# An attention and mixer kernel: one more start-up tile, a weight piece moved, and a small add put on GpSimd

## The chip, the cores and the metric

The kernel runs on one core of one Trainium2 chip. The metric is device time in microseconds for one execution. Three runs of the kernel before took 833.48, 834.04 and 835.19 us; the median is 834.04 us. The profile comes from one execution of its own, which took 833.98 us; the span from its first to its last instruction is 832.2 us, and 1.8 us lie around it.

## What is computed

Windowed attention over 8 batches, 8 heads, 576 positions and 64 channels a head, followed by a mixer with two dense parts. Cut to what matters:

```python
scores = (q @ k.T) / 8                       # every (batch, head)
mask   = 0 <= i - j < 64                     # each row sees at most 64 keys
attn   = softmax(where(mask, scores, -1e9))  # divides by (row sum + 1e-09)
x      = (attn @ v), heads side by side      # 8 x 576 x 512, float32
h      = relu(x.T @ w_tok1) @ w_tok2         # over the positions: 576 -> 256 -> 576
u      = x + h.T
out    = u + relu(u @ w_ch1) @ w_ch2         # over the channels: 512 -> 1536 -> 512
```

[...]

## The kernel before

**Stages.** The attention is cut into 36 tiles of 128 rows. Two batches make nine tiles, and a tile holds two blocks of 64 positions. While tile i is finished, tile i+1 goes through its softmax and tile i+2 has its scores computed, all in one loop over i from -1 to 36. The channel part of the mixer follows and is almost TensorE alone. Products of 32-bit accuracy are made of pairs of rounded numbers, a high part (`xhi`, `w1hi`, `t2hi`, `hhi`) and the rest (`xlo`, `w1lo`, `t2lo`, `hlo`), so a value is split before TensorE uses it.

**One tile.** TensorE (PE) computes the scores `s` (line 274, function `qk`). The scores of one tile take two buffers, and these are free again when the softmax of the tile before has read its own. VectorE (DVE) adds the mask and takes the row maximum, in eight instructions of line 289; four make `softmax(i, 0)` and four `softmax(i, 1)`. ScalarE (ACT) takes the exponentials and the row sums `sum` (line 297). TensorE transposes them into `pp` (line 304), ACT copies this to `pt` (line 306), and TensorE multiplies by `v` into `xp` (line 316, function `av`). Function `recip` makes `ri`, the reciprocal of the row sums, and `norm` (line 330) multiplies `xp` by it on DVE. `split_x` makes `xhi` on ACT and `xlo` on GpSimd (POOL, line 104). `tok1` (line 361) multiplies the split rows by `w_tok1` into `h`; a batch needs five of these tiles. When a batch is complete, ACT takes `hhi` (line 372) and DVE `hlo` (line 381), and the pieces of `tok2` (lines 402 and 409) follow in later tiles. The two buffers of `h` are free for the next batch when `hlo` has been taken.

**Weights.** The 28 first pieces of the weights are converted inside the loop, at most one a tile, as the table `JOBS` says. Pieces 0 to 3 are `w_tok1` (320 columns), 4 to 6 `w_tok2`, the rest `w_ch1` and `w_ch2` (384 columns). A piece is loaded by SyncE's queue (`job_load`), goes through lines 196, 198 and 199 on DVE (`job_convert_a`) and through 208, 210 and 211 on DVE and an add of line 213 on POOL into `w` (`job_convert_b`). Some tiles later `job_finish` splits it: the high part on ACT, the rest on POOL, but on DVE for `w_tok2` (line 104 again).

**Order.** Each engine works its instructions off in the order in which the program writes them. The constant `N_START` sets the order within a tile. In tiles below it, both halves of the next softmax stand at the tile's start, both halves of the exponentials follow one another, waiting pieces are finished before `tok1`, and the conversion stands whole at the tile's end. In tiles from `N_START` on, the second half of the softmax, of the exponentials and the two halves of a conversion are spread over the tile. `N_START` is 6: tiles 0 to 5 have the first manner. Tile 7 runs `tok1` for two tiles (`TOK1_SLOW`), the fifth and the sixth, and needs their `xhi` and `xlo`; `tok2` needs all seven pieces of `w_tok1` and `w_tok2` finished from tile 7 on.

Of the kernel before, what the change touches and what calls it, by code (L numbers as in the profile page):

```python
# [16 lines left out]
ALU = mybir.AluOpType  # L17
# [9 lines left out]
TPP = 9  # L27
# [12 lines left out]
N_FIRST = 28  # L40


JOBS = {i: 1 if 0 <= i < 7 or i == 12 or i > 6 and i % TPP not in (0, 3, 5) else 0 for i in range(-1, 37)}
PIECES = {7: (0, 2), 22: (1, 0), 23: (1, 0), 31: (1, 0), 32: (1, 0), 33: (1, 0), 34: (1, 0), 35: (3, 0), 36: (2, 1)}

TOK1_FROM, TOK1_SLOW, TOK2_FROM = 2, 7, 7

N_START = 6

NX = 4  # L50
NCHUNK = TOK // CHUNK
# [32 lines left out]
def mixer_kernel(ctx: ExitStack, tc: tile.TileContext, qh, kh, vh, wt1, wt2, wc1, wc2, out):  # L84
    nc = tc.nc
# [13 lines left out]
    def split(eng_hi, eng_lo, hi, lo, src):  # L99
        if eng_hi is nc.scalar:  # L100
            nc.scalar.copy(hi, src)  # L101
        else:
            eng_hi.tensor_copy(hi, src)
        eng_lo.tensor_sub(lo, src, hi.bitcast(F32))  # L104
# [18 lines left out]
    with ExitStack() as actx:  # L123
# [8 lines left out]
        def load_k(i):  # L132
            p, t = divmod(i, TPP)
            if t in (0, 4):
                b = 2 * p + (t == 4)
                kbs[b] = pq.tile([P, NBLK + 1, H // 2, BLK], F32, name=f"k{b}", tag="k", bufs=2)
                if b != 0:
                    nc.sync.dma_start(kbs[b], kh[b])

        def load_q(i):  # L140
            qr = pq.tile([P, H // 2, 2, BLK], F32, name=f"q{i}", tag="q", bufs=5)
            nc.sync.dma_start(qr, qh[i])
            loaded[i] = [qr, None]

        def load_v(i):
            vt = pq.tile([P, 2, H, D], F32, name=f"v{i}", tag="v", bufs=3)
            nc.sync.dma_start(vt, vh[i])
            loaded[i][1] = vt
# [89 lines left out]
        def job_convert_b():  # L238
            if to_convert_b:
                n, part = to_convert_b.pop(0)  # L240
                to_finish.append((n, to_f32_b(*part)))
# [3 lines left out]
        def job_finish():  # L245
            if to_finish:
                n, w = to_finish.pop(0)
                finished.add(n)
                src, hi, lo, o, m = jobs[n]
                if hi is None:  # L250
                    nc.sync.dma_start(w2_dram[:, o:o + m], w)
                else:
                    eng = nc.vector if src is wt2 or n >= N_FIRST else nc.gpsimd
                    split(nc.scalar, eng, hi[:, o:o + m], lo[:, o:o + m], w)
                    if src is wt1 and o + m == 5 * DT:
                        for c, r in enumerate((top, bottom)):
                            nc.gpsimd.tensor_copy(t1z[r, c], t1lo[r, 4 * DT:].bitcast(F32))
# [34 lines left out]
        def softmax_exp(i, u):  # L292
            e = e_sb[i, u]
            nm, sm = st[i]
            for h in range(4):
                g = 2 * h + u
                nc.scalar.activation(e[:, h], e[:, h], AF.Exp, bias=nm[:, g:g + 1], scale=-1.0,  # L297
                                     accum_out=sm[:, g:g + 1])
# [22 lines left out]
        def recip(i):  # L321
            _, sm = st.pop(i)
            ri = pa.tile([P, H], F32, name=f"ri{i}", tag="ri", bufs=2)
            nc.vector.scalar_tensor_tensor(out=ri, in0=sm, scalar=1e-9, in1=sm, op0=ALU.add, op1=ALU.max)
            nc.vector.reciprocal(ri, ri)
            return ri

# [61 lines left out]
        def tok2(b, half, ct, hh):  # L389
            assert len(finished) >= 7  # L390
            p, odd = divmod(b, 2)
            base = p * TPP + (5 if odd else 0)
            s0, n = (0, 256) if half == 0 else (256, 320)
            up = ps.tile([P, 512], F32, name=f"up{b}_{half}_{ct}", tag=up_tags[0][0], bufs=up_tags[0][1])
            up_tags.append(up_tags.pop(0))
            cs = slice(ct * P, (ct + 1) * P)
            segs = [(base + 2 * half + j, ident, j * P) for j in range(2)]
            if half == 1:

                segs.append((p * TPP + 4, swapped if odd else ident, 256))  # L400
            for j, (i, perm, o) in enumerate(segs):
                nc.tensor.matmul(up[:, o:o + P], xs[i][:, cs], perm,  # L402
                                 start=(j == 0), stop=False, is_transpose=True, skip_group_check=True)
            k = 0
            for tt in range(NTT):
                hi, lo = hh[tt]
                for hx, w in ((hi, t2hi), (hi, t2lo), (lo, t2hi)):
                    k += 1
                    nc.tensor.matmul(up[:, :n], hx[:, cs], w[:, tt * S + s0:tt * S + s0 + n],  # L409
                                     start=False, stop=(k == 6), skip_group_check=True)  # L410
            if ct == 0:
                ust[b, half] = pa.tile([P, NCT, 320], F32, name=f"u{b}_{half}", tag="ust", bufs=2)
            us = ust[b, half]
            nc.scalar.copy(us[:, ct, :n], up[:, :n])
            if ct == NCT - 1:
                stores.append((us, b * S + s0, n))
                if b >= B - 2:
                    store_u()
# [28 lines left out]
        def run_pieces(k):  # L447
            for _ in range(min(k, len(pieces))):
                tok2(*pieces.pop(0))
# [22 lines left out]
        for i in range(-1, NT + 1):  # L472
            if 0 <= i and i + 2 < NT:
                load_v(i + 2)
            if 3 <= i + 3 < NT:
                load_q(i + 3)
            if i + 4 < NT:
                load_k(i + 4)
            store_u()
            n_jobs = JOBS[i]  # L480
            if i == NT - 1:
                up_tags += [("s", 2), ("pt", 2)]
            have = len(pieces)
            n_pieces = PIECES.get(i, (1, 1) if i >= TOK2_FROM else (0, 0))
            pts = []
            if 0 <= i < NT:
                pts.append(pt_transpose(i, 0))
                if i < NT - 1:
                    pts.append(pt_transpose(i, 1))
            if i + 1 < NT:  # L490
                softmax(i + 1, 0)
            if i < N_START:
                softmax(i + 1, 1)
            if 0 <= i < NT:
                ri = recip(i)
            if i > N_START:
                while to_finish:
                    job_finish()
            for n in tok1_plan.get(i + 1, ()):
                last_use = n - NX + ((n - NX) % TPP == 4)  # L500
                if n < i and last_use not in tok1_plan.get(i, ()):
                    split_x(n)
            if i + 1 < NT:
                softmax_exp(i + 1, 0)
            run_pieces(min(have, n_pieces[0]))
            have = min(have, len(pieces))
            if i >= N_START:
                for _ in range(n_jobs):
                    job_convert_a()
            if i == NT - 1:  # L510
                pts.append(pt_transpose(i, 1))
            if N_START <= i < NT - 1:
                softmax(i + 1, 1)
            if i < N_START:
                softmax_exp(i + 1, 1)
                while to_finish:
                    job_finish()
            for n in tok1_plan.get(i, ()):
                tok1(n)
            if N_START <= i < NT - 1:  # L520
                softmax_exp(i + 1, 1)
            if i >= N_START:
                for _ in range(n_jobs):
                    job_convert_b()
            if 0 <= i < NT:
                norm(i, av(i, pts), ri)
            finish_h_low()
            if i < N_START:
                for _ in range(n_jobs):
                    job_convert_a()  # L530
                    job_convert_b()
            if i + 2 < NT:
                qk(i + 2)
            for n in tok1_plan.get(i + 1, ()):
                if n not in xhl:
                    split_x(n)
            run_pieces(min(have, n_pieces[1]))
            while to_load and len(to_convert) < 2 and i < NT - 2:
                job_load()
            if i == NT - 1:  # L540
                while to_convert or to_convert_b or to_finish:
                    job_convert_a()
                    job_convert_b()
                    job_finish()
                qctx.close()
                pu = uctx.enter_context(tc.tile_pool(name="pu", bufs=1, side="right", reuse_waits="tile"))
                ul = {0: load_u(0, pu)}
# [396 lines left out]
```

## Time and profile before

| what | value |
|---|---|
| median of three runs | 834.04 us |
| time of the profiled execution | 833.98 us |
| its span | 832.2 us |
| PE busy | 812.4 us, 98% |
| DVE busy | 508.7 us, 61% |
| ACT busy | 337.5 us, 41% |
| POOL busy | 105.9 us, 13% |
| PE busy from 0 to 65 us | 50.97 us |
| PE busy from 65 to 250 us (rest of the attention) | 184.62 us |
| mean granted TensorE clock | 0.993 |

A row of the profile names the line of the kernel, the engine, the operation, the tile written and the tiles read, and its start and length. The number in brackets behind it is how long its engine sat idle before it, and what ended that. A busy share is a mean over stages with different limits: the first 65 us of this kernel look unlike all that follows, and times below are counted from the span's start. Tile 0 begins at about 8 us and tile 7 ends at about 65 us.

### The profile page before, as it was taken

The numbers are of one execution on the slowest core, as the hardware profiler recorded it, in microseconds if no ns is written. First come the engines' busy times: TensorE is split into PE (matmuls) and PEld (weight loads), VectorE is DVE, ScalarE is ACT, GpSimd is POOL, SyncE is SP. The second block draws the span as 40 slices with busy tenths as digits, with TensorE's granted clock in tenths as the row PEclk, the third lists the DMA queues.
The fourth block names the chain that finished last, engine by engine and source line by source line (L and its number), as shares of the span: only waits on it lengthen the run. The fifth ranks groups of instructions, "written<-read, shape, count | busy, mean of one in ns | idle before, by whom it ended". The sixth has DMA issues, their size and how long they took to land.

```text
span 832.2 us, 15257 instructions
## 1 busy us (share of the span) xinstructions
PE 812.4 (98%) x5860; PEld 678.7 (82%) x5860; DVE 508.7 (61%) x1372; ACT 337.5 (41%) x1014; POOL 105.9 (13%) x110
## 2 busy tenths in 40 slices
PE   7879999999999999999999999999999999999998
PEld 5658888888888878888888888878888878888886
DVE  5987977788782993774435535267625277525252
ACT  7868888888874440331212202033202032202020
POOL 3533443443430000000000000000000000000000
PEclk9979999999999999999999999999999999999999
DMA  9847778588536538633605442424543334532002
GB/s 348 276 138 240 230 249 270 188 274 287 191 122 192 179 85 242 203 112 114 202 1 196 170 190 89 139 91 165 167 184 110 119 112 172 173 150 89 1 1 101
DMA packets 69672, 136.51 MB, mean 164 GB/s; under 512 B 7008, under 2 KB 39264, under 8 KB 67680
## 3 DMA queue, kind: packets, MB, share of 16 engines
q1 hardware_dynamic: 67488, 133.71, 47.4%
q10 hardware_dynamic: 2112, 1.84, 0.7%
q8 instruction: 46, 0.75, 0.4%
q14 instruction: 26, 0.21, 0.1%
HBM read 104.66 MB, written 30.87 MB: 163 GB/s over the span
## 4 chain that ended last, share of the span: by engine, by line
PE 82%; DVE 10%; ACT 3%; issue 2%; DMA 2%; POOLq 0%; SPq 0%; POOL 0%; DVEq 0%; ACTq 0%
PE gp L843 19%; PE op L631 11%; PE gp L623 8%; PE up L409 5%; PE h L361 5%; PE op_4a L631 4%; PE op_2b L631 4%; PE op_2a L631 4%; PE op_0b L631 4%; PE op_0a L631 4%; PE op_4b L631 4%; PE s L274 3%; PE xp L316 3%; PE pp L304 3%; PE up L402 2%
## 5 line engine op out<-in xcount | busy, mean ns | idle before, releaser
L843 PE MATMUL gp<-m,w1hi 128*128 128x512 f32 x504 | 155.4, 389 | 0.7 <-DVE x L851 0.7
L297 ACT ACTIVATE e<-e,nm 128x128 f32<-128x128 f32 x288 | 112.3, 397 | 12.4 <-DVE nm L289 12.3
L843 PEld LDWEIGHTS gp<-m,w1hi 128*128 128x128 f32 x504 | 94.5, 188 | 20.9 <-DVE x L851 1.5
L843 PE MATMUL gp<-m,w1lo 128*128 128x512 f32 x252 | 98.0, 389 | 0.0
L610 ACT ACTIVATE ghi<-x 128x512 fp32r<-128x512 f32 x54 | 34.2, 632 | 119.8 <-DVE x L853 68.3
L289 DVE CUSTOM_DVE_ANT_0 e<-s,mask 128x128 f32<-128x128 f32 x288 | 65.3, 284 | 11.3 <-PE s L274 11.1
L847 ACT COPY x<-gp 128x512 f32<-128x512 f32 x18 | 10.4, 578 | 143.7 <-PE gp L843 143.7
L611 DVE SCALAR_TENSOR_TENSOR glo<-x,ghi 128x512 fp32r<-128x512 f32 x54 | 37.4, 692 | 38.1 <-ACT ghi L610 38.1
L610 ACT ACTIVATE ghi<-gp 128x512 fp32r<-128x512 f32 x50 | 29.9, 598 | 70.3 <-PE gp L623 70.3
L623 PE MATMUL gp<-ulo,w1hi 128*128 128x512 f32 x144 | 56.0, 389 | 0.0
L623 PE MATMUL gp<-uhi,w1hi 128*128 128x512 f32 x144 | 56.0, 389 | 0.0
L297 ACT ACTIVATION_READ_ACCUMULATOR e<-e,nm 128x1 f32 x288 | 56.0, 195 | 0.0
L623 PE MATMUL gp<-uhi,w1lo 128*128 128x512 f32 x144 | 56.0, 389 | 0.0
L843 PEld LDWEIGHTS gp<-m,w1lo 128*128 128x128 f32 x252 | 47.3, 188 | 9.9
L274 PE MATMUL s<-k,q 64*64 64x128 f32 x1152 | 43.2, 280 | 10.4 <-DVE nm L289 4.1
L611 DVE SCALAR_TENSOR_TENSOR glo<-gp,ghi 128x512 fp32r<-128x512 f32 x50 | 34.4, 689 | 25.4 <-ACT ghi L610 25.3
L631 PE MATMUL op<-glo,w2hi 128*128 128x512 f32 x128 | 49.8, 389 | 0.0
L631 PE MATMUL op<-ghi,w2hi 128*128 128x512 f32 x128 | 49.8, 389 | 0.0
L631 PE MATMUL op<-ghi,w2lo 128*128 128x512 f32 x128 | 49.8, 389 | 0.0
L316 PEld LDWEIGHTS xp<-v,pt 128*64 128x64 f32 x1152 | 36.6, 138 | 13.3 <-ACT e L297 9.4
L104 POOL TENSOR_TENSOR xlo<-x,xhi 128x512 fp32r<-128x512 f32 x32 | 41.3, 1292 | 38.8 <-ACT xhi L101 38.5
L274 PEld LDWEIGHTS s<-k,q 64*64 64x64 f32 x1152 | 33.4, 135 | 14.5 <-issue 10.6
(160 smaller groups left out, 1835.0 us busy)
## 6 DMA issues: line engine op xcount, KB each, us to landing
v<-vh SPq DMA_DIRECT2D x36, 512.0 KB, 4.1
w1hi<-w1s SPq DMA_DIRECT2D x18, 896.0 KB, 4.6
w1lo<-w1s SPq DMA_DIRECT2D x18, 896.0 KB, 6.4
raw<-wc SPq DMA_DIRECT2D x32, 384.0 KB, 4.4
q<-qh SPq DMA_DIRECT2D x36, 256.0 KB, 4.6
k<-kh SPq DMA_DIRECT2D x7, 1280.0 KB, 7.8
out<-uf SPq DMA_DIRECT2D x35, 256.0 KB, 2.8
uf<-u_dram SPq DMA_DIRECT2D x8, 1024.0 KB, 9.2
```

Of the source, the lines that this page charges most:

```text
L104: eng_lo.tensor_sub(lo, src, hi.bitcast(F32))
L274: nc.tensor.matmul(so, qt[r, j, half], kbs[b][r, n:n + 2, j], start=True, stop=True)
L289: nc.vector.tensor_tensor_reduce(out=e[:, h], in0=s[:, h], in1=mk, scale=-scale, scalar=MAX_F32, op0=ALU.add, op1=ALU.min, accum_out=nm[:, ...
L297: nc.scalar.activation(e[:, h], e[:, h], AF.Exp, bias=nm[:, g:g + 1], scale=-1.0, accum_out=sm[:, g:g + 1])
L316: nc.tensor.matmul(xp[half * BLK:(half + 1) * BLK, h], pts[h % 2][:, h // 2, half * BLK:(half + 1) * BLK], vt[:, half, h], start=True, sto ...
L361: nc.tensor.matmul(h_ps[b][tt], w[:, o + tt * P:o + (tt + 1) * P], x, start=first and n == 0, stop=last and n == len(combos) - 1)
L409: nc.tensor.matmul(up[:, :n], hx[:, cs], w[:, tt * S + s0:tt * S + s0 + n], start=False, stop=(k == 6), skip_group_check=True)
L610: nc.scalar.activation(hi, src, AF.Relu)
L611: nc.vector.scalar_tensor_tensor(out=lo, in0=src, scalar=0.0, in1=hi.bitcast(F32), op0=ALU.max, op1=ALU.subtract)
L623: nc.tensor.matmul(gp, w[:, w1_at(ft, ct)], x[:, ct], start=(k == 0), stop=(k == 3 * NCT - 1))
L631: nc.tensor.matmul(op, w[:, ct, ft], x[:, cols], start=(first and k == 0), stop=(last and k == 3 * len(gs) - 1), skip_group_check=not (fir ...
L843: nc.tensor.matmul(b, w[:, at], c[:, h, t], start=(n < 4 and k == 0), stop=(k == 5), skip_group_check=True)
```

## The change

Three edits. The first makes tile 6 a tile of the first manner (`N_START` goes from 6 to 7), and adds a `job_finish` to tile 7, so that pieces 5 and 6 of the weights, which tile 7 finished together, are finished in tile 6 and tile 7. The second takes the conversion out of tile 7 and gives one to tile 18, which had none; the pieces between them are converted by one tile's place later. The third makes the first step of `recip`, the add of 1e-9 to the 128 by 8 sums, an instruction of POOL instead of DVE; the reciprocal stays on DVE.

```diff
-JOBS = {i: 1 if 0 <= i < 7 or i == 12 or i > 6 and i % TPP not in (0, 3, 5) else 0 for i in range(-1, 37)}
+JOBS = {i: 1 if 0 <= i < 7 or i in (12, 18) or i > 7 and i % TPP not in (0, 3, 5) else 0 for i in range(-1, 37)}
-N_START = 6
+N_START = 7
         def recip(i):
             _, sm = st.pop(i)
             ri = pa.tile([P, H], F32, name=f"ri{i}", tag="ri", bufs=2)
-            nc.vector.scalar_tensor_tensor(out=ri, in0=sm, scalar=1e-9, in1=sm, op0=ALU.add, op1=ALU.max)
+            nc.gpsimd.tensor_scalar_add(ri, sm, 1e-9)
             nc.vector.reciprocal(ri, ri)
             return ri
...
             if i + 1 < NT:
                 softmax_exp(i + 1, 0)
+            if i == N_START:
+                job_finish()
             run_pieces(min(have, n_pieces[0]))
```

On DVE, from the reciprocal of tile 6 (`ri_843`, now `ri_848`) to the multiplication `x` of the same tile. `c` and `r` belong to piece 6 of the weights, `e_1` is the second half of tile 7's softmax. First before, then now (now the second half of the softmax stands ahead of these rows, and the conversion is the last of them).

```order
L325 RECIPROCAL ri_843<-ri_843 128x8
L196 TENSOR_SCALAR c_854<-raw_710 128x384
L198 TENSOR_SCALAR c_854<-c_854 128x384
L199 TENSOR_SCALAR c_854<-c_854 128x384
L289 ISA e_1_858,nm_836<-s_1_799,mask_90 128x128
...
L208 SCALAR_TENSOR_TENSOR c_854<-raw_710,c_854 128x384
L210 TENSOR_SCALAR r_875<-c_854 128x384
L211 SCALAR_TENSOR_TENSOR r_875<-raw_710,r_875 128x384
L330 TENSOR_TENSOR x_898<-xp_881,ri_843 128x512
L381 SCALAR_TENSOR_TENSOR hlo_0_900<-h_0_449,hhi_0_867 128x512
L381 SCALAR_TENSOR_TENSOR hlo_1_902<-h_1_450,hhi_1_869 128x512
```

```order
L325 RECIPROCAL ri_848<-ri_848 128x8
L104 TENSOR_TENSOR t2lo<-w_793,t2hi 128x384
L330 TENSOR_TENSOR x_890<-xp_873,ri_848 128x512
L381 SCALAR_TENSOR_TENSOR hlo_0_892<-h_0_449,hhi_0_869 128x512
L381 SCALAR_TENSOR_TENSOR hlo_1_894<-h_1_450,hhi_1_871 128x512
L196 TENSOR_SCALAR c_896<-raw_710 128x384
L198 TENSOR_SCALAR c_896<-c_896 128x384
L199 TENSOR_SCALAR c_896<-c_896 128x384
L208 SCALAR_TENSOR_TENSOR c_896<-raw_710,c_896 128x384
L210 TENSOR_SCALAR r_900<-c_896 128x384
L211 SCALAR_TENSOR_TENSOR r_900<-raw_710,r_900 128x384
```

The six conversion steps moved behind the multiplication and the two `hlo`, and a `t2lo`, which waits for ACT, moved ahead of them.

On POOL, two pieces of the difference: tiles 3 and 4, then tiles 6 and 7. `w_901` (`w_876` before) is piece 6, `xlo_852` and `xlo_925` (`xlo_847` and `xlo_923`) the low parts of tiles 5 and 6, which `tok1` in tile 7 reads.

```order
 L213 TENSOR_TENSOR w_481<-r_480,c_476 128x320
+L324 TENSOR_SCALAR ri_536<-sum_421 128x8
 L104 TENSOR_TENSOR xlo_540<-x_474,xhi_539 128x512
 L104 TENSOR_TENSOR t1lo<-w_481,t1hi 128x320
 L213 TENSOR_TENSOR w_583<-r_582,c_578 128x320
+L324 TENSOR_SCALAR ri_638<-sum_525 128x8
```

```order
 L213 TENSOR_TENSOR w_793<-r_792,c_788 128x384
-L104 TENSOR_TENSOR xlo_847<-x_786,xhi_846 128x512
-L213 TENSOR_TENSOR w_876<-r_875,c_854 128x384
-L104 TENSOR_TENSOR xlo_923<-x_898,xhi_922 128x512
...
+L324 TENSOR_SCALAR ri_848<-sum_733 128x8
+L104 TENSOR_TENSOR xlo_852<-x_786,xhi_851 128x512
+L213 TENSOR_TENSOR w_901<-r_900,c_896 128x384
+L104 TENSOR_TENSOR xlo_925<-x_890,xhi_924 128x512
+L324 TENSOR_SCALAR ri_955<-sum_837 128x8
```

In tiles 3 and 4 the add stands ahead of `xlo`. In tile 7, and from there on, it stands behind it. `w` of piece 6 still stands ahead of tile 6's `xlo`, but it now waits for a conversion that ends the tile.

## The prediction

> **What bounds the kernel now.** I read the busy shares and slices first, then the windows, then TensorE's own timeline.
>
> ```profile
> PE 812.4 (98%) x5860; PEld 678.7 (82%) x5860; DVE 508.7 (61%) x1372; ACT 337.5 (41%) x1014; POOL 105.9 (13%) x110
> PE   7879999999999999999999999999999999999998
> PEclk9979999999999999999999999999999999999999
> ```
>
> TensorE is the bound, except in the first four slices (20.8 us each), where the third also has a lower clock. By a window of the rest of the attention (columns: length, then busy time and count of PE, PEld, DVE, ACT, POOL, then PE's granted clock, DMA share, GB/s):
>
> ```profile
> 65.00:250.00 185.00, 184.62 (x2580) 161.15 (x2578) 151.50 (x639) 161.01 (x600) 76.03 (x66) 1.00 0.69 228
> ```
>
> From 65 us on PE works 184.62 of 185 us. Whatever is gained or lost before 65 us is kept to the end; whatever is only moved behind it counts when PE is made to wait. So I ask when PE reaches one fixed point, the scores of tile 9 (`qk(9)`), now at 62.15. PE around tiles 6 and 7:
>
> ```profile
> 45.55 1.15 PE L316 MATMUL xp<-v,pt 128*64 128x64 f32 x32 [0.30 <-ACT pt L306]
> 49.03 0.69 PE L274 MATMUL s<-k,q 64*64 64x128 f32 x4 [2.33 <-issue]
> 52.44 1.97 PE L274 MATMUL s<-k,q 64*64 64x128 f32 x28 [2.72 <-DVE nm L289]
> ...
> 57.39 0.63 PE L361 MATMUL h<-xlo,t1z 128*128 128x512 f32 x1
> 57.81 0.63 PE L361 MATMUL h<-xhi,t1hi 128*128 128x512 f32 x1
> ...
> 60.50 0.40 PE L361 MATMUL h<-xlo,t1hi 128*128 128x512 f32 x1
> 60.73 0.40 PE L361 MATMUL h<-xhi,t1lo 128*128 128x512 f32 x1
> ...
> 62.15 1.10 PE L274 MATMUL s<-k,q 64*64 64x128 f32 x32
> ```
>
> PE is empty from 46.70 to 52.44 but for four matmuls, because `qk(8)` needs buffers that tile 7's softmax frees late. And `h` matmuls start 0.42 us apart at 57.4, but 0.23 at 60.5: the clock.
>
> ```profile
> 44.98:48.40 3.42, 1.41 (x34) 1.04 (x32) 3.25 (x10) 0.87 (x3) 0.17 (x1) 1.00 0.10 38
> 48.40:58.60 10.20, 6.85 (x46) 5.67 (x47) 9.32 (x38) 7.71 (x28) 4.33 (x4) 0.50 0.50 156
> ...
> 4.02:7.44 3.42, 2.08 (x37) 1.41 (x35) 1.07 (x11) 0.74 (x4) 1.39 (x5) 1.00 1.01 346
> ```
>
> The clock was 0.50 from 48.4 to 58.6. It fell after 3.4 us in which PE worked 1.41 us; after a stretch with 2.08 of 3.42 us it had not fallen.
>
> **The add on POOL, tiles 1 to 4.** DVE in tiles 2 to 4, POOL beside it, and the group of the adds:
>
> ```profile
> 27.46 0.28 DVE L289 CUSTOM_DVE_ANT_0 e<-s,mask 128x128 f32<-128x128 f32 x1
> ...
> 29.15 0.61 DVE L324 SCALAR_TENSOR_TENSOR ri<-sum 128x8 f32<-128x8 f32 x1
> 29.79 0.20 DVE L325 RECIPROCAL ri<-ri 128x8 f32<-128x8 f32 x1
> ...
> 31.78 1.05 DVE L208 SCALAR_TENSOR_TENSOR c<-raw,c 128x320 int32<-128x320 int32 x1
> 33.71 0.28 DVE L289 CUSTOM_DVE_ANT_0 e<-s,mask 128x128 f32<-128x128 f32 x1
> ```
> ```profile
> 28.46 1.28 POOL L104 TENSOR_TENSOR xlo<-x,xhi 128x512 fp32r<-128x512 f32 x1
> 31.46 1.02 POOL L104 TENSOR_TENSOR t1lo<-w,t1hi 128x320 fp32r<-128x320 f32 x1 [1.73 <-ACT t1hi L101]
> ```
> ```profile
> L324 DVE SCALAR_TENSOR_TENSOR ri<-sum 128x8 f32<-128x8 f32 x36 | 29.6, 822 | 0.0
> ```
>
> Eight numbers a row should not take 822 ns. In tile 3 the add runs from 29.15 to 29.76 and POOL's `xlo` from 28.46 to 29.74: the add sits out POOL's subtraction. Line 208 sits out `t1lo` in the same way (31.78 to 32.83, against 31.46 to 32.48). With the add on POOL ahead of `xlo`, DVE's reciprocal comes 0.64 us earlier (29.15 for 29.79).
>
> [...]
>
> But the 0.64 us brings DVE earlier to `t1lo`, which doesn't move with it: it hangs on the eight exponentials that follow the softmax. Then 210 or 211 waits there instead. From ACT's rows below, a softmax at 0 gives the first exponential at 0.38 and the high part at 3.47; its 0.44 us and 0.07 to POOL put `t1lo` at 3.98 to 5.00; then about 0.6 for what is left of lines 210 and 211. A tile can't be shorter than 5.6 us; now it is 6.25 (27.46 to 33.71). So 0.6 a tile is the most, tile 1 meets `t1lo` already at its end (0.4), and tile 4 has two half copies of `xhi` on ACT. Ends: 0 (the wait is only moved) and 4 x 0.64 = 2.6; I take the middle, **1.3 us**. Tile 0's sums are ready long before, tile 5 waits for ACT anyway: nothing there.
>
> **Tile 6 in the first manner.** Tile 5 is the model, since it too finishes a `t2` piece:
>
> ```profile
> 40.29 0.28 DVE L289 CUSTOM_DVE_ANT_0 e<-s,mask 128x128 f32<-128x128 f32 x1
> 44.29 0.56 DVE L104 TENSOR_TENSOR t2lo<-w,t2hi 128x384 fp32r<-128x384 f32 x1 [1.18 <-ACT t2hi L101]
> 44.77 0.68 DVE L330 TENSOR_TENSOR x<-xp,ri 128x512 f32<-128x512 f32 x1
> 45.37 0.35 DVE L196 TENSOR_SCALAR c<-raw 128x384 int32<-128x384 int32 x1
> 48.00 0.28 DVE L289 CUSTOM_DVE_ANT_0 e<-s,mask 128x128 f32<-128x128 f32 x1
> ...
> 54.34 1.28 DVE L381 SCALAR_TENSOR_TENSOR hlo<-h,hhi 128x512 fp32r<-128x512 f32 x2
> 55.54 0.28 DVE L289 CUSTOM_DVE_ANT_0 e<-s,mask 128x128 f32<-128x128 f32 x1
> ```
> ```profile
> 40.67 0.40 ACT L297 ACTIVATE e<-e,nm 128x128 f32<-128x128 f32 x1 [0.91 <-DVE nm L289]
> 43.76 0.50 ACT L101 CAST t2hi<-w 128x384 fp32r<-128x384 f32 x1
> ```
> ```profile
> 53.91 1.00 POOL L213 TENSOR_TENSOR w<-r,c 128x384 f32<-128x384 f32 x1 [3.46 <-DVE r L211]
> 55.16 1.28 POOL L104 TENSOR_TENSOR xlo<-x,xhi 128x512 fp32r<-128x512 f32 x1 [0.25 <-ACT xhi L101]
> ```
>
> On the old clock, tile 6 begins at 48.00. Its softmax is whole by 49.7, so `qk(8)` runs at 49.8 instead of 52.44: 2.6 us won there. But the chain behind it is longer: `t2lo` 4.00 after the start (52.29), `norm` at 52.77, the two `hlo` 0.60 later until 54.57, the conversion 2.63 (45.37 to 48.00) until 57.2. Tile 8's softmax stands there at 57.2; now it is at 55.54. Before, `xlo` of tile 6 ran at 55.16. Now POOL does piece 6's `w` first: 0.1 after the conversion's end, 57.1 or 57.2, then 1.0, then `xlo` 1.28, until 59.4 to 59.5. `tok1` needs it for its last five `h` matmuls. PE reaches these at about 56.5 and **waits some 2.9 us**. That is what is late next. The five take 4 x 0.23 to the last start, `xp(7)` follows 0.33 later (60.73 to 61.06 now) and `qk(9)` 1.09 after that (62.15): 59.45 + 0.92 + 0.33 + 1.09 = 61.8. Against 62.15, **0.4 us** won, and with the 1.3 from above 1.7. The other ways to `qk(9)` are shorter: `ri` of tile 7 behind `xlo` at 59.8, the second `t2lo` and tile 8's softmax end by 61.2.
>
> **The clock in tiles 6 and 7.** This 1.7 us is for full clock. PE would be empty for about 2 us before `qk(8)`, 1.7 before `h` (which needs the buffers `hlo` frees, at 53.8), and 2.9 before the last five. The row that fell had 2 of 3.4 us empty, so I expect a fall, and the last gap puts it right before work that now sets the end. Price: PE resumed at 52.44 and the clock came back at 58.6, 6.2 us later. At half clock 6.2 us of such work would be 3.1 lost; a fall that comes early and is over by then costs 0. I take the middle, **1.6 us lost**.
>
> [...]
>
> **Tiles 8 to 36 and the moved piece.** Here the add stands behind `xlo` on POOL, and DVE's reciprocal waits for it, with the conversion and the second softmax half queued behind:
>
> ```profile
> 85.57 1.29 POOL L104 TENSOR_TENSOR xlo<-x,xhi 128x512 fp32r<-128x512 f32 x1 [0.25 <-ACT xhi L101]
> ```
> ```profile
> 85.76 1.12 DVE L324 SCALAR_TENSOR_TENSOR ri<-sum 128x8 f32<-128x8 f32 x1
> ...
> 91.58 0.29 DVE L289 CUSTOM_DVE_ANT_0 e<-s,mask 128x128 f32<-128x128 f32 x1 [0.15 <-PE s L274]
> 137.96 0.69 DVE L330 TENSOR_TENSOR x<-xp,ri 128x512 f32<-128x512 f32 x1 [3.17 <-PE xp L316]
> ```
> ```profile
> 88.04 1.39 PE h L361 x6
> ```
> ```profile
> 2.92 0.14 POOL L166 MEMSET mask<- 64x64 f32 x1
> ```
>
> These are POOL, DVE, the chain of waits (PE's next `h` at 88.04) and POOL at the start. `xlo` ends at 86.86 and the old add at 86.88, so the order of events stays; what comes on top is the add's length and the way back to DVE. No row has either: from 0.14 (the small MEMSET) to 1.0 (`w`) for the add, 0.1 for the way. Nearest in size is the MEMSET: 0.25 a tile. DVE's own idle of 0.15 a tile, and the 1.2 us from the end of `xlo` to the `h` that reads it, hide it; without cover it is 0.25 x 28 = 7 us. Tile 18's new conversion is 2.6 us on DVE, under the 3.17 us that DVE waits there; its load, and those of the nine pieces between, pass one more tile's loads on SP, and its `w` and split find POOL and ACT free. I cost this at 0.
>
> **Sum.** -1.3 - 0.4 + 1.6 = -0.1 on the profiled 833.98 (0.06 below the median): **833.9 us**.
>
> **Rivals.** (1) The clock stays up, or is back before 59 us: for it, that each gap is shorter than the present one of 5.7 us; against it, the row at 44.98. 833.98 - 1.7 = 832.3. (2) Slower: the add on POOL costs like `w`, 1.0 us, and with 0.1 for the way DVE's loop from `norm` over `xhi`, `xlo`, add and reciprocal grows by 1.1 a tile, 0.15 of it idle now. In the runs of tiles that all convert (10 to 13, 15 to 20 with the new one, 24 to 26) that is 13 x 0.95 = 12.4, less 1.2 us of cover at the start of each run: 8.8. Time: 833.9 + 8.8 = 842.7. It decides once the add takes more than about 0.5 us (13 x 0.45 less 3.6 is 2.3). Against it: POOL's short rows. (3) The change doesn't do what it says: the 0.64 us only moves to `t1lo`, nothing is won in tiles 1 to 4, and the clock is low as forecast: 833.98 - 0.4 + 1.6 = 835.2.
>
> **Chances.** Forecast 0.56, rival 1 0.22, rival 2 0.11, rival 3 0.11. 0.2% is 1.7 us, about what can be told from no change. The forecast's own range is 832.6 to 835.2. Rival 1 is at the bound; I count 0.17 of it as faster, and 0.07 of the forecast where the lock gives more. Slower are rival 2, and 0.07 of forecast and rival 3 at the clock's full 3.1. So faster 0.24, same 0.58, slower 0.18, and a range of 831.8 to 836.0, which leaves out most of rival 2 and a tail of rival 1.
>
> **What would show it.** Line 324 as a POOL row of 0.1 to 0.3 us and softmax of tile 7 near 46.7; `qk(8)` about 48.5; a gap of PE of 2 to 3 us that ends with POOL's `xlo`; `qk(9)` between 60.4 and 63.6; a clock below 0.6 somewhere from 47 to 62. It is wrong if the clock stays at 1.00, if tile 6 doesn't begin 0.7 to 2 us earlier, or if PE has idle time between 65 and 250 us beyond the present 0.4.

## The result, and the profile after

The changed kernel takes 837.94 us (median of five runs, 837.84 to 839.56), against 834.04 us (832.53 to 835.19) for the kernel before. The ratio is 1.0052, 95% interval 1.0036 to 1.0067: it is slower by about 4 us, beyond the 0.2% that the prediction gave as about what can be told from no change. I had forecast 833.9 us and a range of 831.8 to 836.0.

The profiled execution has a span of 836.3 us, 4.1 more than before. From the page of the changed kernel, the busy line and two rows of slices, and from its windows the rest of the attention (columns as before):

```profile
PE 817.5 (98%) x5860; PEld 680.7 (81%) x5860; DVE 482.2 (58%) x1336; ACT 337.4 (40%) x1014; POOL 113.6 (14%) x146
PE   8979999999999999999999999999999999999998
PEclk9989999999999999999999999999999999999999
...
65.00:250.00 185.00, 182.80 (x2516) 157.79 (x2514) 127.82 (x606) 159.56 (x597) 81.89 (x93) 1.00 0.67 224
```

DVE is busy 26.5 us less, the first two slices are fuller than before, and the clock of the third is higher. But PE, which had worked 184.62 of these 185 us, now works 182.80 and gets through 2516 matmuls instead of 2580. That is where the time goes. The multiplications of line 330 cut the attention into stages. Tile 0, tile 8 and the last tile, before:

```profile
12.16 0.69 DVE L330 TENSOR_TENSOR x<-xp,ri 128x512 f32<-128x512 f32 x1 [0.26 <-PE xp L316]
...
70.28 0.69 DVE L330 TENSOR_TENSOR x<-xp,ri 128x512 f32<-128x512 f32 x1 [1.67 <-PE xp L316]
...
248.60 0.69 DVE L330 TENSOR_TENSOR x<-xp,ri 128x512 f32<-128x512 f32 x1 [0.54 <-PE xp L316]
```

And after:

```profile
12.94 0.69 DVE L330 TENSOR_TENSOR x<-xp,ri 128x512 f32<-128x512 f32 x1 [1.23 <-PE xp L316]
...
68.46 0.69 DVE L330 TENSOR_TENSOR x<-xp,ri 128x512 f32<-128x512 f32 x1 [1.44 <-PE xp L316]
...
252.59 0.68 DVE L330 TENSOR_TENSOR x<-xp,ri 128x512 f32<-128x512 f32 x1
```

Tile 0 comes 0.78 us later, tiles 0 to 8 are 2.60 us shorter (55.52 for 58.12), and tiles 8 to 35 are 5.81 us longer (184.13 for 178.32). From the last multiplication to the end it is 583.6 us before and 583.7 after. 0.78 - 2.60 + 5.81 + 0.1 is the 4.1. The start went better than forecast, the rest lost what I had costed at nothing. The 0.78 can't be put down to the change: the kernel before, profiled again, reaches tile 0 at 12.60, and the kernels below, which do nearly the same until there, between 12.03 and 13.75 (the three above 13.5 are those whose clock was halved for 3.4 us between 8.3 and 12.2).

PE around tiles 6 and 7 of the changed kernel, and the add as the view of the tile `ri` gives it (shortest, median and longest in ns):

```profile
47.53 0.43 PE L274 MATMUL s<-k,q 64*64 64x128 f32 x4 [2.33 <-issue]
48.42 1.97 PE L274 MATMUL s<-k,q 64*64 64x128 f32 x28 [0.45 <-DVE ri L325]
...
57.89 0.50 PE L361 MATMUL h<-xlo,t1hi 128*128 128x512 f32 x1 [1.57 <-POOL xlo L104]
60.33 1.10 PE L274 MATMUL s<-k,q 64*64 64x128 f32 x32
```
```profile
L324 POOL TENSOR_SCALAR ri<-sum x36: 232/233/242, 11.2 to 249.6; 128x8 f32<-128x8 f32 x36
```

Most of the signs I had named are there: the softmax of tile 7 at 46.51, `qk(8)` at 48.42, a gap of PE that ends with `xlo` (1.57 us, where I gave 2 to 3), `qk(9)` at 60.33 (a hair earlier than the 60.4 to 63.6 I gave), the add at 0.233 us. What I had not expected stands in the view of waits of DVE between 65 and 250 us (what was waited for; us in total, times, longest):

```profile
DVE ri L325 <- POOL ri L324: 41.9, 27, 2.9
```

Much of this is not new, since the old add on DVE spent the same time as busy time, next to the same `xlo` (1.06 us in the rows below). So I look at what a tile does with it, DVE first and POOL behind it. Lines 196 to 211 are DVE's steps of the conversion, which turns the 64-bit numbers of a weight piece into 32-bit ones. Before, tile 11 to 12:

```profile
90.74 0.68 DVE L330 TENSOR_TENSOR x<-xp,ri 128x512 f32<-128x512 f32 x1
92.43 1.06 DVE L324 SCALAR_TENSOR_TENSOR ri<-sum 128x8 f32<-128x8 f32 x1
93.53 0.20 DVE L325 RECIPROCAL ri<-ri 128x8 f32<-128x8 f32 x1
93.65 0.31 DVE L196 TENSOR_SCALAR c<-raw 128x384 int32<-128x384 int32 x1
...
94.87 0.28 DVE L289 CUSTOM_DVE_ANT_0 e<-s,mask 128x128 f32<-128x128 f32 x1
...
97.13 0.68 DVE L330 TENSOR_TENSOR x<-xp,ri 128x512 f32<-128x512 f32 x1
```
```profile
92.19 1.28 POOL L104 TENSOR_TENSOR xlo<-x,xhi 128x512 fp32r<-128x512 f32 x1 [0.28 <-ACT xhi L101]
94.72 1.02 POOL L104 TENSOR_TENSOR w1lo<-w,w1hi 128x384 fp32r<-128x384 f32 x1 [1.25 <-ACT w1hi L101]
```

After, the end of tile 11 to 12 and the whole of tile 12 to 13:

```profile
92.97 1.18 DVE L199 TENSOR_SCALAR c<-c 128x384 int32<-128x384 int32 x1
...
96.37 0.68 DVE L330 TENSOR_TENSOR x<-xp,ri 128x512 f32<-128x512 f32 x1
99.42 0.20 DVE L325 RECIPROCAL ri<-ri 128x8 f32<-128x8 f32 x1 [1.53 <-POOL ri L324]
99.54 1.16 DVE L196 TENSOR_SCALAR c<-raw 128x384 int32<-128x384 int32 x1
103.71 0.68 DVE L330 TENSOR_TENSOR x<-xp,ri 128x512 f32<-128x512 f32 x1
```
```profile
92.92 1.02 POOL L104 TENSOR_TENSOR w1lo<-w,w1hi 128x384 fp32r<-128x384 f32 x1 [0.84 <-ACT w1hi L101]
...
97.78 1.29 POOL L104 TENSOR_TENSOR xlo<-x,xhi 128x512 fp32r<-128x512 f32 x1 [0.24 <-ACT xhi L101]
99.15 0.23 POOL L324 TENSOR_SCALAR ri<-sum 128x8 f32<-128x8 f32 x1
99.47 1.02 POOL L104 TENSOR_TENSOR w1lo<-w,w1hi 128x384 fp32r<-128x384 f32 x1
```

Counted from `x`, the reciprocal came 2.79 us later before and 3.05 now, in both tiles: 0.26, very near the 0.25 of the prediction. But the tile grows by more. Tile 11 to 12 takes 7.31 us now (from 89.06) for 6.39, and tile 12 to 13 takes 7.34 for 6.51: 0.92 and 0.83. (The texts below set 7.34 against 6.39, 0.95, which are neighbouring tiles.)

The rest is a step of the conversion. In tile 11 to 12 it is line 199. Counted from `x` it stands 0.26 later than before, and POOL's `w1lo` 0.12 earlier; so it now starts 0.05 behind `w1lo`, and takes 1.18 us instead of 0.36. In the next tile it is line 196, 1.16 us for 0.31: it starts 0.07 behind `w1lo` and ends 0.2 behind its end. I say that it sits out `w1lo`, and call it a lock where a DVE step begun beside a POOL instruction ends only behind that one's end. What holds it up no row shows.

Before, `w1lo` ran under the second half of the softmax (from 94.72; the step at 94.87 takes its 0.28), which it doesn't hold up. Line 199 had begun 0.33 ahead of it, at 94.39, and took its 0.36. Once a tile is in the lock, `w1lo` comes earlier too: in tile 12 to 13 it stands directly behind the add, 3.10 us after `x` instead of 3.99. Behind tile 8, nine tiles of the changed kernel have one of the lines 196, 198 and 199 sit out `w1lo`, at 1.05 to 1.22 us; the kernel before has none.

### The profile page after: what moved, and what is told of

It reads as the page before. It is cut to its first block, busy times and chain, and to the rows that moved or that the text cites. A ratio compares the mean times of both kernels' runs of the same rounds, so it can differ in the third digit from the quotient of the medians.

```text
span 836.3 us, 15228 instructions
## 1 busy us (share of the span) xinstructions
PE 817.5 (98%) x5860; PEld 680.7 (81%) x5860; DVE 482.2 (58%) x1336; ACT 337.4 (40%) x1014; POOL 113.6 (14%) x146
## 4 chain that ended last, share of the span: by engine, by line
PE 62%; DVE 5%; issue 1%; DMA 1%; ACT 0%; POOLq 0%; POOL 0%; DVEq 0%; SPq 0%; ACTq 0%
PE gp L845 19%; PE op L633 11%; PE gp L625 8%; PE op_4a L633 4%; PE op_2b L633 4%; PE op_2a L633 4%; PE op_0b L633 4%; PE op_0a L633 4%; PE op_4b L633 4%; PE up L409 1%; DVE glo L613 1%; DVE w2lo L104 1%; DVE r L211 0%; DMA u_dram<-u 0%; DVE c L208 0%
## 5 line engine op out<-in xcount | busy, mean ns | idle before, releaser
L274 PE MATMUL s<-k,q 64*64 64x128 f32 x1152 | 46.7, 283 | 6.5 <-issue 2.3
L274 PEld LDWEIGHTS s<-k,q 64*64 64x64 f32 x1152 | 35.2, 137 | 12.6 <-issue 7.8
```

What stands on the lines that cost most here:

```text
L274: nc.tensor.matmul(so, qt[r, j, half], kbs[b][r, n:n + 2, j], start=True, stop=True)
```

## The experiments

All ran beside the kernel before, and each ratio is to the runs of it on the same chip; its median there is 833.28 to 834.04 us, so medians of different rows can be compared only to that. The stages are read from line 330's start times as above, each in one profiled execution.

| kernel | median us | ratio (95%) | tiles 0 to 4 | 4 to 8 | 8 to 35 |
|---|---|---|---|---|---|
| before | 834.04 | 1 | 24.17 | 33.95 | 178.32 |
| before, profiled again | 833.90 | | 24.16 | 33.21 | 178.34 |
| changed | 837.94 | 1.0052 (1.0036 to 1.0067) | 21.65 | 33.87 | 184.13 |
| add only | 836.61 | 1.0036 (1.0024 to 1.0048) | 21.64 | 33.74 | 182.85 |
| tile 6 and the moved piece, no add on POOL | 835.74 | 1.0022 (1.0013 to 1.0032) | 24.15 | 33.63 | 179.12 |
| tile 6 only | 834.89 | 1.0009 (1.0000 to 1.0018) | 24.17 | 34.21 | 178.30 |
| changed, add ahead of `w` | 832.79 | 0.9995 (0.9985 to 1.0005) | 21.65 | 33.87 | 179.07 |
| changed, no add | 832.32 | 0.9986 (0.9975 to 0.9997) | 21.91 | 33.55 | 178.20 |
| changed, add twice | 844.85 | 1.0130 (1.0114 to 1.0145) | 21.67 | 33.85 | 191.59 |
| before, add ahead of `w` | 832.33 | 0.9982 (0.9973 to 0.9990) | 21.66 | 34.43 | 178.39 |
| tile 6, add ahead of `w`, piece not moved | 832.73 | 0.9991 (0.9982 to 1.0000) | 21.66 | 34.63 | 178.35 |
| changed, add between `w` and `xlo` | 831.51 | 0.9969 (0.9957 to 0.9981) | 21.66 | 35.35 | 178.22 |
| changed, add ahead of `w`, piece in tile 21 | 831.87 | 0.9982 (0.9972 to 0.9993) | 21.66 | 33.84 | 178.37 |
| changed, `w1lo` later | 838.49 | 1.0062 (1.0050 to 1.0074) | 21.66 | 35.32 | 184.79 |
| changed, `w1lo` cut short | 832.40 | 0.9991 (0.9979 to 1.0004) | 21.65 | 33.84 | 179.26 |

### Which edit

**The add alone**, in the kernel before:

```diff
-            nc.vector.scalar_tensor_tensor(out=ri, in0=sm, scalar=1e-9, in1=sm, op0=ALU.add, op1=ALU.max)
+            nc.gpsimd.tensor_scalar_add(ri, sm, 1e-9)
```

> The kernel before with the third edit alone: the add of 1e-9 on GpSimd, tile 6 and the conversions as before. Theory Q (the queue): the loss lies in tiles 8 to 36, where the add stands behind `w` and `xlo` in POOL's queue, so that DVE's reciprocal, and with it the rest of the tile, starts late. It needs no other edit: 838 us (836.5 to 840), DVE waiting over 25 us for line 324 between 65 and 250 us. Theory M (the moved piece and tile 6): the loss comes from tile 18's new conversion and the pieces converted a tile later; then the add alone wins its 1.3 us of the first tiles and gives 832 to 834 us.

It took 836.61 us, within theory Q's range: 2.5 us won in tiles 0 to 4 and 4.5 lost behind tile 8. The add on POOL is enough for most of the loss.

**The first two edits without the add**, the changed kernel with the add back on DVE:

> The changed kernel with the add back on DVE: the first two edits alone. Theory Q: nothing is lost behind tile 8, and the start keeps what the tile 6 edit wins: 833.3 us (832.0 to 834.6), the scores of tile 9 at 61 to 62 us, PE busy again about 184.6 us of 65 to 250 us. Theory M: 837 to 839 us, with DVE or PE waiting longer around tile 18 and in the tiles whose piece has moved.

835.74 us, outside theory Q's range and short of theory M's. Tiles 8 to 35 lose 0.80, all of it from tile 18 to tile 21 (7.94 us for 7.22, 6.99 for 6.25, then 5.61 for 6.28). **The first edit alone** (`N_START` 7 and the `job_finish`, the table of conversions as before) separates these two edits:

> The kernel before with the first edit alone: tile 6 in the first manner, the add on DVE, the conversion still in tile 7 and none in tile 18. Compared with the run that had both of the first two edits (835.7 us, tiles 8 to 35 0.8 us longer than before): if tile 18's new conversion is what lengthened them, through `w1lo`, which now meets the conversion steps of tiles 19 and 20 on DVE, the norms of tiles 8 to 35 are 178.3 us apart again and the time is 833 to 835; if it is something else of the tile 6 edit, they stay near 179.1 and the time near 835.7.

Tiles 8 to 35 are 178.30 again, and the time 834.89 us. So the 0.80 belongs to tile 18's conversion. Its piece brings a `w1lo` into tile 19, where before there was none. In the run without the add on POOL, DVE and POOL there:

```profile
143.55 1.10 DVE L199 TENSOR_SCALAR c<-c 128x384 int32<-128x384 int32 x1
...
150.15 1.09 DVE L198 TENSOR_SCALAR c<-c 128x384 f32<-128x384 f32 x1
```
```profile
143.42 1.01 POOL L104 TENSOR_TENSOR w1lo<-w,w1hi 128x384 fp32r<-128x384 f32 x1 [0.79 <-ACT w1hi L101]
```

Line 199 takes 1.10 us instead of 0.36, and line 198 in the next tile 1.09, beside the next `w1lo` (150.00 to 151.02). I had checked the 2.6 us of conversion against DVE's wait, and not what a piece does one tile later on POOL. Tile 6 in the first manner wins nothing by itself: its ratio is 1.0009, and 4 to 8 (34.21) lies among the other kernels. What the two edits lose together beyond the 0.80, about 1 us by the ratio, isn't behind tile 8; this profile reached tile 0 only at 13.55, its clock halved from 8.3 to 11.7, and what the other executions did before tile 8 was not seen.

### The place in the queue

**The add ahead of `w`.** The add of tile i+1 is issued in tile i, right behind its last exponential:

```diff
+        def recip_add(i):
+            ...
+            nc.gpsimd.tensor_scalar_add(ri_of[i], sm, 1e-9)
...
             if N_START <= i < NT - 1:
                 softmax_exp(i + 1, 1)
+                recip_add(i + 1)
             if i >= N_START:
                 for _ in range(n_jobs):
                     job_convert_b()
```

> The changed kernel, but in tiles from 8 on the add for the tile's sums is issued to POOL one place earlier, right behind the second half of the exponentials, so that it stands ahead of `w` and `xlo` in POOL's queue; still on GpSimd, still 0.23 us. Theory Q: the wait of DVE for line 324 is gone (under 5 us in all), tiles that convert are 6.3 to 6.5 us long again, and what the start won is kept: 832.3 us (831.3 to 833.5). [...]

832.79 us: 5.06 of the 5.81 us behind tile 8 are back, with the same 0.23 us on the same engine. The 0.75 that stay are tile 18's conversion again, as the run with the piece in tile 21 shows. I had taken the queue and `w1lo` beside a conversion step as if only one of them could be at work; that was the wrong question, as the runs further down show.

**No add at all** (the 1e-9 is left out):

> The changed kernel without the add: the reciprocal on DVE reads the sums themselves, so the 1e-9 is left out of the computation. Neither engine does the add. Theory Q: no wait for POOL at the reciprocal, DVE shorter by line 324's 29.6 us of before: 832 us (831 to 833), and PE 65 to 250 us as before. [...] It is also the bound of what any place for the add can win over the changed kernel.

832.32 us with 178.20: an add placed well costs nothing that can be told from having none.

**The add between `w` and `xlo`**, with `recip_add(i + 1)` one step further down, behind `job_convert_b`:

> The changed kernel with the add between the two places tried so far: in tiles from 8 on it stands behind `w` but ahead of `xlo` in POOL's queue. It tells which of the two instructions ahead of the add costs. DVE has about 0.7 + 4 x 0.21 = 1.5 us of work (the multiplication, half a softmax) between the last conversion step and the reciprocal; `w` and the add take 1.0 + 0.3. If it is `xlo`, which needs DVE's multiplication and ACT's cast first, the wait for line 324 is gone and the time is as with the add ahead of both: 832.8 us (832 to 833.8). If `w` costs a good part, 834.5 us or more.

831.51 us, below the 832 where I had the range begin, 0.3% faster than the kernel before and the lowest of all, though the intervals of the next best overlap its own. So `w` ahead of the add costs nothing, and of the two `xlo` is the one that must not stand ahead of it. DVE and POOL of this kernel:

```profile
97.42 0.69 DVE L337 TENSOR_TENSOR x<-xp,ri 128x512 f32<-128x512 f32 x1
99.30 0.20 DVE L332 RECIPROCAL ri<-ri 128x8 f32<-128x8 f32 x1
99.41 1.07 DVE L196 TENSOR_SCALAR c<-raw 128x384 int32<-128x384 int32 x1
...
101.61 0.29 DVE L289 CUSTOM_DVE_ANT_0 e<-s,mask 128x128 f32<-128x128 f32 x1
...
102.03 0.90 DVE L208 SCALAR_TENSOR_TENSOR c<-raw,c 128x384 int32<-128x384 int32 x1
...
104.00 0.69 DVE L337 TENSOR_TENSOR x<-xp,ri 128x512 f32<-128x512 f32 x1
```
```profile
98.67 0.23 POOL L326 TENSOR_SCALAR ri<-sum 128x8 f32<-128x8 f32 x1
98.99 1.28 POOL L104 TENSOR_TENSOR xlo<-x,xhi 128x512 fp32r<-128x512 f32 x1
101.49 1.03 POOL L104 TENSOR_TENSOR w1lo<-w,w1hi 128x384 fp32r<-128x384 f32 x1 [1.22 <-ACT w1hi L101]
```

The wait on `xlo` has not gone; it has moved from the add to line 196 (1.07 us, until 100.48, for an `xlo` that ends at 100.27). But `w1lo` falls for the most part under the softmax again; line 208 sits out only its end (0.90 for 0.55), and the tile, 12 to 13, is 6.58 us long (6.51 before). This place of the add also avoids tile 18's loss (178.22).

### The lock

**The add twice**, for tiles from 8 on, measures how hard the loop of DVE and POOL is:

> The changed kernel with the add done twice on GpSimd in tiles from 8 on (2e-9 is added there instead of 1e-9; nothing else differs). It measures the slope: 0.23 us and some 0.06 to 0.1 us between two instructions more in each tile. Theory Q: the tiles that convert run in a closed loop (`w`, `xlo`, add, reciprocal, conversion, second softmax half, conversion, `w`), so each of about 11 to 16 of them grows by the full 0.3: 841 to 843 us against 837.9. The price as I put it in the prediction's rival 2 (nothing below about 0.5 us, since it is covered) would give 838 to 839.

844.85 us, above both: my 11 to 16 tiles were too few. The tiles of 7.34 grow to 7.65, by the 0.23 and the 0.08 between two instructions, so these tiles take on the whole of what POOL does between `xlo` and the reciprocal. Two tiles that had been 6.48 jump by a full 1.0 us to 7.49 and 7.51. Their lines 198, which had not been beside `w1lo`, now sit it out (1.06 and 1.08 us). A loss that comes in a step of that size points to a lock.

**`w1lo` later.** The split of a finished piece is written behind the first half of the exponentials:

```diff
-            if i > N_START:
-                while to_finish:
-                    job_finish()
...
                 softmax(i + 1, 1)
+            if i > N_START:
+                while to_finish:
+                    job_finish()
```

> The changed kernel with the add where the change puts it, but with the split of a finished weight piece (`w1hi` on ACT, `w1lo` on POOL) written behind the first half of the exponentials instead of ahead of it, in tiles from 8 on. `w1lo` then stands some 2 us later and no longer directly behind the add. It splits the loss of a converting tile, 7.34 against 6.39 us: the trace gives about 0.26 to the later reciprocal and about 0.86 to line 196, which sits out `w1lo` (1.16 against 0.31 us). If the lock by `w1lo` is what makes the tile long, the converting tiles fall to 6.4 to 6.6 us and the time to 833.5 us (832.8 to 834.8), though the add still waits behind `xlo`; if the wait for the add does it, 837 us or more; if `w1lo` meets line 208 in its new place instead, something between.

838.49 us; nothing is won. By the words of the expectation, 837 or more, this speaks for the wait, but the rows say otherwise. DVE and POOL:

```profile
101.80 0.31 DVE L196 TENSOR_SCALAR c<-raw 128x384 int32<-128x384 int32 x1
103.66 1.31 DVE L208 SCALAR_TENSOR_TENSOR c<-raw,c 128x384 int32<-128x384 int32 x1
```
```profile
103.56 1.00 POOL L104 TENSOR_TENSOR w1lo<-w,w1hi 128x384 fp32r<-128x384 f32 x1 [1.91 <-ACT w1hi L101]
```

Line 196 is short again, and line 208 now sits out `w1lo` (1.31 for 0.55). The lock has only moved, and I had put the price of that too low (something between); so this run couldn't separate it from the wait.

**`w1lo` cut short** does. The subtraction takes 16 of 384 columns, and the rest of `w1lo` is set to zero at the start:

```diff
+        nc.gpsimd.memset(w1lo.bitcast(F32), 0.0)
...
-                    split(nc.scalar, eng, hi[:, o:o + m], lo[:, o:o + m], w)
+                        nc.scalar.copy(hi[:, o:o + m], w)
+                        nc.gpsimd.tensor_sub(lo[:, o:o + 16], w[:, :16], hi[:, o:o + 16].bitcast(F32))
```

> The changed kernel with `w1lo` cut short: for the 16 pieces of `w_ch1` converted inside the attention, GpSimd takes the low part of 16 of 384 columns only, and the rest of `w1lo` stays zero from a memset at the start (so the low part of `w_ch1` is left out of the product; the matmuls run all the same). The add still waits behind `xlo`, but no 1 us instruction of POOL follows it. If `w1lo`'s lock on DVE, wherever it falls, makes up 0.8 of the 0.95 us that a converting tile lost, these tiles fall from 7.34 to about 6.5 us and tiles 8 to 35 to 178.3 to 179.5: 833 us (832 to 834.5). If the wait for the add alone is enough, the tiles stay above 7 and the time at 836.5 or more.

832.40 us, and 179.26 for tiles 8 to 35. The wait for the add, by the view of waits of this kernel, is what it was in the changed one:

```profile
DVE ri L330 <- POOL ri L329: 42.0, 27, 2.6
```
```profile
94.60 0.68 DVE L335 TENSOR_TENSOR x<-xp,ri 128x512 f32<-128x512 f32 x1
97.64 0.20 DVE L330 RECIPROCAL ri<-ri 128x8 f32<-128x8 f32 x1 [1.40 <-POOL ri L329]
97.77 0.31 DVE L197 TENSOR_SCALAR c<-raw 128x384 int32<-128x384 int32 x1
101.08 0.68 DVE L335 TENSOR_TENSOR x<-xp,ri 128x512 f32<-128x512 f32 x1
```

The reciprocal comes 3.04 us after `x`, as in the changed kernel (3.05), and the tile, 12 to 13 again, is 6.48 us long instead of 7.34. Behind tile 8 no step of a conversion is longer than 0.56 us. So the add behind `xlo` makes the reciprocal 0.26 us late, which alone costs a tile 0.1 at most (6.49 for the 6.39 of before in tile 11 to 12, 6.48 for 6.51 in the next); and from there DVE's conversion meets `w1lo` and sits it out, which costs the rest. Of the 5.81 us behind tile 8, 0.94 stay with the wait alone and 4.87 need the lock as well, tile 18's 0.7 to 0.8 among them. (The cut also takes 0.8 us a tile of POOL's own time, 0.22 for 1.02, but POOL has no work waiting there.)

### Without the other edits, and another tile for the piece

**The kernel before with the add ahead of `w`**, nothing else, and **the same with tile 6 in the first manner and no piece moved**:

> The kernel before with the add on GpSimd and nothing else, but in tiles from 7 on issued one place earlier, ahead of `w` and `xlo` in POOL's queue. Theory Q: the start wins 2.7 us, as in the run with the add alone, and nothing is lost behind it: 831 us (830 to 832.2), faster than both kernels. If the tile 6 edit were needed to keep what the start wins, or if the early add cost something behind tile 8: 832.8 us or more.

> The changed kernel with the add issued early, but without the second edit: the conversion stays in tile 7, tile 18 has none. The run with the early add and both edits took 832.8 us, with 0.75 us lost at tiles 18 to 20. If tile 18's conversion costs that and the conversion in tile 7 costs nothing: 832.0 us. If tile 7's conversion delays the scores of tile 9 (60.1 us in that run) by more than 0.75: 833 us or more.

832.33 and 832.73 us. The first is 0.1 us above the range I gave, the second between my two figures. In both, tiles 8 to 35 (178.39 and 178.35) are as expected; what is short lies in tiles 4 to 8 (34.43 and 34.63, against 33.84 to 33.87 in the profiles of the changed kernel and four of its variants, but 35.32 and 35.35 in two more), which one profile each doesn't settle. The first shows that the add on POOL, well placed, makes the kernel faster with neither of the other edits.

**The piece in tile 21** instead of 18, with the add ahead of `w`:

> The changed kernel with the add issued ahead of `w` and `xlo`, and with the conversion that left tile 7 put into tile 21 instead of tile 18. Tile 21 is of the kind of tile 12, which converts in every kernel here; tile 18 follows the tile that takes the low parts of `h`. If the place is what costs, tiles 8 to 35 are 178.3 us again instead of 179.1, and the start keeps its 2.6 us: 832.0 us (831.2 to 832.8). If any tile with a conversion more costs as much: 832.8 us.

831.87 us and 178.37: tile 18's loss is gone. Not every tile without a conversion is equally free.

**The kernel before once more**, for a second profile:

> The kernel before once more, unchanged, for a second profile. The first has a halved clock from 48.4 to 58.6 us and a mean clock of 0.993, where most of its other executions have 0.996. If the clock's place is a matter of chance, this profile has it low for a shorter time or elsewhere, and the scores of tile 9 not at 62.15 us but up to 1 us away; tiles 8 to 35 take 178.3 us as before.

The clock, by windows of this second profile of the kernel before, and of the one profiled execution of the kernel with the add between `w` and `xlo`:

```profile
50.64:57.49 6.85, 4.61 (x39) 4.11 (x40) 6.33 (x27) 4.35 (x14) 2.52 (x3) 0.51 0.57 201
```
```profile
8.60:11.95 3.35, 3.35 (x40) 2.98 (x39) 1.41 (x13) 2.12 (x11) 0.24 (x1) 0.50 1.04 411
49.60:52.95 3.35, 3.08 (x29) 2.35 (x20) 1.70 (x4) 3.10 (x11) 0.53 (x1) 0.50 0.70 279
59.60:63.30 3.70, 3.70 (x62) 3.13 (x64) 1.46 (x9) 2.15 (x9) 0.23 (x1) 0.54 0.07 10
```

The same kernel had its clock low for 10.2 us in one execution and 6.85 in another, and `qk(9)` came at 62.15 and 61.84.

## Why the prediction was wrong

**The step that failed is the last: tiles 8 to 36, and the moved piece, costed at 0.** They cost 5.81 us. The first half of that step was right: I had the add's length and way to DVE as 0.25 a tile, and in most tiles the reciprocal came 0.26 to 0.30 later. That the size fits so well is in part luck, since its parts were off and made up for each other: the add took 0.233 us, not 0.14, the way from it to the reciprocal 0.04, not 0.1, and 0.08 passed between `xlo` and the add, which I had left out. Behind the `x` of seven tiles (13, 14, 22, 23, 31, 32 and 34) it came 1.4 to 1.8 us later; with `w1lo` cut short it does so too, and all of tiles 8 to 35 lose only 0.94.

What failed is how I covered the delay. I set it against 0.15 of idle time on DVE and 1.2 us up to the `h` that reads `xlo`, as if a delay could only shift what follows. But what followed was aligned with POOL: in the kernel before, `w1lo` fell under softmax steps, which it doesn't disturb (0.28 us beside it), and with the delay it fell on a step of the conversion, which sits it out (1.16 and 1.18 us for 0.31 and 0.36). At most 0.1 of shift and 0.82 to 0.85 of lock make up the 0.83 to 0.95 by which the tiles shown grow. I had the rows that show such a lock (the old add, 822 ns on average, and line 208 beside `t1lo`) and had used them only for tiles 1 to 4.

**A lock that I looked for in too few lines.** In tiles 1 to 4 I let line 210 wait for `t1lo`. Lines 196 to 199 are `tensor_scalar` instructions with one input like it, and in tiles 8 to 36 I didn't ask what POOL does beside them. The kernel before shows one of them held up, by an `xlo` that ran from 113.08 to 114.53:

```profile
113.42 1.33 DVE L198 TENSOR_SCALAR c<-c 128x384 f32<-128x384 f32 x1
```

It is 0.36 us long where POOL does nothing, and 1.33 to 1.39 in three more tiles. Line 196 too has one input, and takes 1.16 us instead of 0.31 beside `w1lo`. The softmax steps are not held up (0.29 us for the one at 101.61 in the best kernel, with `w1lo` running from 101.49).

**The moved piece.** Of the 5.81 us, 0.7 to 0.8 are tile 18's conversion (179.07 against 178.37 with the piece in tile 21; 179.12 against 178.30 without the add on POOL). The 2.6 us on DVE are hidden, as I said; in these places the `w1lo` that follows is not.

**The add in tiles 0 to 4: right mechanism, size too small.** I took 1.3 us, the middle of 0 and 2.6. Measured is 24.17 - 21.65 = 2.52, and every kernel with the add on POOL has it within 0.03. The wait at `t1lo` came as I had described it. Line 210 in tile 3 of the changed kernel, with `t1lo` from 31.01 to 31.97:

```profile
31.27 0.88 DVE L210 TENSOR_SCALAR r<-c 128x320 int32<-128x320 int32 x1
```

It is 0.33 us long without company. But this takes the place of a wait that the kernel before had there too (line 208, 1.05 for 0.49), and the tile is 5.53 us long (27.07 to 32.60), close to the 5.6 that I had worked out as its shortest. So the working was good for 0.4 + 3 x 0.6 = 2.2 us, and taking the middle between that and nothing is what made the term too small. Rival 3 is out.

**Tile 6 in the first manner: 0.4 forecast, nothing that can be measured.** Tiles 4 to 8 are 33.21 and 33.95 in the two profiles of the kernel before, and 33.55 to 35.35 in those of the kernels with this edit: they differ by more than 0.4 among themselves. The clock seems to be part of that: the two above 35 are the only ones in which it was halved twice between tiles 4 and 8, the second time from 58.6 to 62.0 and from 59.8 to 63.2. The steps are as I described them (`qk(8)` at 48.42, then the wait for `xlo`), with a wait of 1.57 instead of 2.9.

**The clock: 1.6 us forecast, no difference found.** A window of the changed kernel's profile:

```profile
48.05:54.80 6.75, 6.24 (x42) 5.09 (x43) 4.48 (x14) 5.00 (x18) 1.27 (x2) 0.50 0.45 168
```

It fell, as I said, but was back before PE's last wait (57.89 - 1.57 = 56.3). The second profile of the kernel before shows that such a fall differs between executions of one kernel (10.2 us and 6.85). I had charged the change for a fall that the kernel before pays too. What the step should have said: a term of either sign that differs from execution to execution, and no reason to put it on one side.

**The rivals.** Rival 2 named the right place and the right sign, and the price was wrong: it made the add's own length decide, from 0.5 us on. At 0.233 us it had cost about 5 us already. Had I followed the 0.26 through the rest of the tile, row by row, and asked at each DVE step what POOL does at that moment, the step to 7.3 us might have shown. The sign I gave for being wrong, idle time of PE between 65 and 250 us beyond 0.4, is the one that came: 2.2 us.

## What to carry to other kernels

When an instruction is handed to another engine, what it is queued behind there can decide, more than how long it is: here 0.23 us behind `xlo` cost 5 us, and the same 0.23 us ahead of it nothing. When an instruction of one engine sits out another engine's, as line 196 does `w1lo` here (1.16 us for 0.31), a delay can't simply be set against idle time; write both engines' rows side by side, shift one by the delay, and look for what now coincides. And a conversion put into a free tile brings its later steps along: look for them one and two tiles further down, on every engine.

## What the runs showed that I had not expected

- Two profiles of the same kernel differ in where and how long the clock is halved (48.4 to 58.6 us, and 50.64 to 57.49). The one profiled execution of the best kernel took 834.39 us, with the clock halved in three places, while its five other executions, with a mean clock of 0.995 to 0.996 for its 0.993, took 831.05 to 831.60: one execution can be 3 us off, three quarters of what the change lost. What sets off a fall the traces don't show.
- The lock shows in both kinds of DVE step: 0.31 to 1.16 us for line 196 with one input, 0.55 to 1.31 for line 208 with two.
- The tiles in the lock pass on all of a further delay: 0.31 us more on POOL made tiles of 7.34 us 7.65 long.
- A DVE wait can disappear from the list of waits and stay in the kernel: in the best kernel DVE waits 1.1 us for the add between 65 and 250 us, where it was 41.9, since line 196 sits out `xlo` instead, as busy time.
